# Fused attention and two MLPs on one core: weight words side by side in 8 KB places, operations over 1024 columns, output chunks later in the order of conversion

## The chip, the cores and the metric

The kernel runs on one core of a Trainium2 chip. The metric is the device time of one execution in microseconds (us), the median of several runs; less is better.

## The reference

Banded attention (window 32, for half of the heads dilated by 4) over 4 x 576 tokens with 8 heads of 64, then two feed-forward layers of 512 to 2048 to 512 over the 2304 tokens, the first with a rational function between its matrices, the second with a leaky ReLU:

```python
attn = softmax(where(mask, scale * q @ k.T, -1e9)); x = attn @ v      # per head, then side by side
h = x @ w_in;  g = P(h) / (Q(h) + 1e-6);  x = g @ w_out                 # layer 1: 512 -> 2048 -> 512
h = x @ w_in;  g = max(h, 0) + alpha * min(h, 0);  out = g @ w_out      # layer 2
```

The weights reach the chip as 64-bit floats (two 32-bit words each), so the kernel has to turn each of them into a 32-bit float first.

## The kernel before

**Tiling.** The 2304 tokens are 6 blocks (n) of 384, the 2048 hidden columns are 16 chunks (c) of 128. The unit of the first layer's loop is a pair J: two chunks of one block, so J = 0 to 7 is block 0, and there are NP = 48. For each pair TensorE forms h (`inproj`, L397, into two PSUM banks "h"), ScalarE and VectorE form g (`rat_1`, L415 to L419, which frees the bank, and `rat_2`, L425 to L430, whose last operation writes g), and TensorE adds it to the block's output (`outproj`, L448) two pairs later. Blocks 1 to 5 work with numbers split in a high and a low part (three products); block 0 works with whole f32 words and needs the weights only converted, not split. Attention runs ahead in 48 groups G, one per pair from J = 0 on, nine before the loop. The second layer follows, with a seven-product scheme over block pairs (from about 560 us on).

**Weights.** A chunk is 128 x 512 values, 128 x 1024 words of 32 bits, 4 KB in each partition. `w_load` brings the chunks of layer 1 into 16 places of 4 KB (the tags `inh0`, `outh0`, `inh2` and so on, which later hold the high parts). `w_convert` takes a pair of chunks, each in its own place, with seven operations: two Abs on ScalarE over 512 columns (L159, they read every second word), one shift on VectorE over 1024 columns (L160), two shift-and-or over 512 (L162) and two and-or over 512 (L167). The results `win`, `wout` are the f32 weights of block 0. `w_split` (L187, L188) makes high and low parts from pair J = 7 on. `w_early` converts eleven pairs of layer 2's weights during J = 16 to 42 and puts them back into DRAM.

**Order.** Nine attention groups run before the loop, and in their steps k = 3 and k = 6 one and two pairs of chunks are converted at a lower priority: in 0, then out 0 and in 2. Each of the pairs J = 0 to 6 then converts two more at its end (`w_next` twice), in the order in 0, out 0, in 2, out 2, in 4, out 4 and so on. The loads are all issued by SyncE's queue (SP), in order: the first 16 chunks before the loop, four more in each of J = 0 to 3, each as soon as the place it goes to has been converted. Every engine works through its instructions in order; a planner settles the orders from program order, priorities and expected readiness, so that an operation may stand earlier or later on its engine than in the program.

**Names.** "In 0" is the pair of input chunks 0 and 1, "out 0" the pair of output chunks 0 and 1. On the page `raw_inh`, `raw_outh` are chunks as loaded, `hl`/`gl` ends mean low parts (in block 0 `gl` is the whole g), `tc` the numerator, `ps_h` the h banks, `ps_y` the output banks.

Of the kernel before, what the change touches and what calls it, by code (L numbers as in the profile page):

```python
# [19 lines left out]
BLK = 384  # L20
# [35 lines left out]
def attn_rational_prelu_kernel(  # L56
# [58 lines left out]
    wt, raw_t, w32_t = {}, {}, {}  # L115
    src = {(1, "in"): w1_in, (1, "out"): w1_out, (2, "in"): w2_in, (2, "out"): w2_out}

    places = [f"{kind}h{c}" for c in range(0, NC, 2) for kind in ("in", "out")]
    n_raw = {1: 0, 2: 0}
    SPARE = (f"inh{NC - 2}", f"outl{NC - 4}")  # L120

    def w_load(*key):


        if key in w_dram:
            t = rawp.tile([128, 2 * DM], F32, tag="raw", name="w32")
# [3 lines left out]
        k = n_raw[key[0]]  # L130
        n_raw[key[0]] += 1
        tag = places[k % NC] if key[0] == 1 else SPARE[k % 2]
        t = wp.tile([128, 2 * DM], U32, tag=tag, name="raw_" + tag)
        nc.sync.dma_start(out=t, in_=src[key[:2]][key[2]].bitcast(U32))
        raw_t[key] = t

    def w_early(layer, kind, c):


        for i in range(2):  # L140
            t = rawp.tile([128, 2 * DM], U32, tag="raw", name="raw")
            nc.sync.dma_start(out=t, in_=src[layer, kind][c + i].bitcast(U32))
            raw_t[layer, kind, c + i] = t
        a = w_convert(layer, kind, c, f"outl{NC - 2}")
        w_dram[layer, kind, c] = dp.tile([128, 2 * DM], F32, name=f"w_dram_{kind}{c}")
        nc.sync.dma_start(out=w_dram[layer, kind, c], in_=a.bitcast(F32))

    def w_convert(layer, kind, c, tag=None):


        if layer == 1 or tag:
            a = wp.tile([128, 2 * DM], U32, tag=tag or f"{kind}l{c}", name=f"w{kind}{c}")
        else:
            a = rawp.tile([128, 2 * DM], U32, tag="u", name="u", bufs=1)
        halves = [slice(i * DM, (i + 1) * DM) for i in range(2)]
        words = [raw_t.pop((layer, kind, c + i)).rearrange("p (f t) -> p t f", t=2) for i in range(2)]
        for i in range(2):
            w32_t[layer, kind, c + i] = a[:, halves[i]]
            nc.scalar.activation(out=a[:, halves[i]].bitcast(F32), in_=words[i][:, 1, :].bitcast(F32), func=AF.Abs, scale=W_BIAS)  # L159
        nc.vector.tensor_scalar(out=a, in0=a, scalar1=3, scalar2=0, op0=ALU.logical_shift_left, op1=ALU.bitwise_or)  # L160
        for i in range(2):
            nc.vector.scalar_tensor_tensor(  # L162
                out=a[:, halves[i]], in0=words[i][:, 0, :], scalar=29, in1=a[:, halves[i]],
                op0=ALU.logical_shift_right, op1=ALU.bitwise_or,
            )
        for i in range(2):
            nc.vector.scalar_tensor_tensor(  # L167
                out=a[:, halves[i]], in0=words[i][:, 1, :], scalar=0x80000000, in1=a[:, halves[i]],
                op0=ALU.bitwise_and, op1=ALU.bitwise_or,
            )  # L170
        raw_t[layer, kind, c] = a
        return a
# [3 lines left out]
    def w_split(layer, kind, c):  # L176


        w = raw_t.pop((layer, kind, c)).bitcast(F32)
        hi = wp.tile([128, 2 * DM], F32R, tag=f"{kind}h{c}", name=f"w{kind}h{c}")  # L180
        k = c + (kind == "out")
        if k == 0 and layer == 1:
            lo = rawp.tile([128, 2 * DM], F32R, tag="u", name="winl0", bufs=1)
        else:
            tag = f"outl{NC - 2}" if k == 0 else f"inl{c}" if k % 2 else f"outl{c - 2}"
            lo = wp.tile([128, 2 * DM], F32R, tag=tag, name=f"w{kind}l{c}")
        nc.scalar.activation(out=hi, in_=w, func=AF.Copy)  # L187
# [308 lines left out]
    def stage(name):  # L496
# [7 lines left out]
    X_TAGS = {
        "B11": ("inh0", f"outl{NC - 2}"), "T2": ("inh2", "outl0"), "B21": ("inh4", "outl2"),
        "T3": ("xh0", "xl0"), "T1": ("xh0", "xl0"), "T4": ("xh1", "xl1"), "B22": ("xh1", "xl1"),
    }
    W_TAGS = (("inh6", "outl4", "inh8", "outl6"), ("inh10", "outl8", "inh12", "outl10"))

    def sub(out, a, b):  # L510
        nc.vector.tensor_tensor(out=out, in0=a, in1=b, op=ALU.subtract)  # L511

    def x_alloc(n, name):
        pool = xp if X_TAGS[name][0][0] == "x" else wp
        st_x[n, name] = [
            pool.tile([128, 2 * BLK], F32R, tag=tag, name=f"st_{name}{s}") for tag, s in zip(X_TAGS[name], "hl")
        ]

    def x_load(n):
# [32 lines left out]
        split(*st_x[n, name], st[name])  # L552

    def st_wload(q):
        t = rawp.tile([128, 2 * DM], F32, tag="raw", name="w32")
        nc.sync.dma_start(out=t, in_=w_dram[2, "in", 2 * q])
        return t

    def st_prep(q, w):
# [8 lines left out]
        ah, al = (wp.tile([128, 2 * DM], F32R, tag=t, name="st_a") for t in tags[:2])  # L568
        sh, sl = (wp.tile([128, 2 * DM], F32R, tag=t, name="st_s")[:, :768] for t in tags[2:])
# [99 lines left out]
    def w_pairs(layer):  # L669
        return [(layer, kind, c) for c in range(0, NC, 2) for kind in ("in", "out")]  # L670

    to_convert = {1: w_pairs(1), 2: [(2, "out", c) for c in range(0, NC, 2)]}
    early = w_pairs(2)[:6] + [(2, "in", c) for c in range(6, NC, 2)]
    to_load = {
        1: [(l, k, c + i) for l, k, c in w_pairs(1) for i in range(2)],
        2: [(l, k, c + i) for l, k, c in to_convert[2] for i in range(1 if (l, k, c) in early else 2)],
    }

# [236 lines left out]
```

## Time and profile before

| | |
|---|---|
| time, median of 3 runs | 913.36 us (911.81 to 914.83) |
| the profiled execution, its own time | 911.72 us |
| its span from first to last instruction | 909.9 us |
| TensorE matmul busy | 893.2 us (98%) |
| VectorE busy | 772.8 us (85%) |
| ScalarE busy | 632.7 us (70%) |
| mean granted TensorE clock | 0.996 of full speed |

PE is TensorE's matmul stream, PEld its weight loads, DVE VectorE, ACT ScalarE, SPq the queue of SyncE that issues the DMAs. A wait is put down to the instruction that released it. A granted clock of 1.00 is 2.4 GHz, 0.50 is 1.2 GHz. Successive rows of one engine overlap by about 0.1 us, since an instruction starts before the last one's results are out; the distance from start to start is what the engine is held for.

### The profile page before, as it was taken

What the parts mean: (1) busy time and instruction counts of PE and PEld (TensorE: products, weight loads), DVE (VectorE), ACT (ScalarE), POOL (GpSimd) and SP (SyncE); (2) the same over time, 40 slices, a digit from 0 to 9 for tenths busy, and PEclk for the clock granted to TensorE, in tenths of its full rate; (3) what the DMA queues carried; (4) which work ended last, traced back from release to release, by engine and by line L of the source; (5) the groups of instructions that cost most, each with busy time, mean ns of one, the idle gap of its engine ahead of it and who ended that gap; (6) DMA issues with size and microseconds to landing.
All of it is one profiled execution on the core that took longest, in us unless ns stands there. A gap on an engine that the chain in (4) does not pass through costs nothing.

```text
span 909.9 us, 14970 instructions
## 1 busy us (share of the span) xinstructions
PE 893.2 (98%) x5682; PEld 789.9 (87%) x5682; DVE 772.8 (85%) x1297; ACT 632.7 (70%) x1357; POOL 0.2 (0%) x4
## 2 busy tenths in 40 slices
PE   7799999999999999999999999999999999999998
PEld 5465568899999999999999999898898898988896
DVE  4999999998889988999999999999986769676652
ACT  5789988778988888898787856555554537553533
POOL 0000000000000000000000000000000000000000
PEclk9899999999999999999999999999999999999999
DMA  9995112213434434442211233232231102210001
GB/s 246 375 358 191 46 44 80 66 45 113 149 115 134 132 104 141 130 157 94 88 48 47 87 124 120 92 104 86 89 116 37 34 24 81 94 47 24 1 1 69
DMA packets 37896, 93.97 MB, mean 103 GB/s; under 512 B 4672, under 2 KB 14400, under 8 KB 37824
## 3 DMA queue, kind: packets, MB, share of 16 engines
q1 hardware_dynamic: 37824, 93.02, 31.5%
q8 instruction: 44, 0.72, 0.3%
q14 instruction: 28, 0.23, 0.1%
HBM read 77.79 MB, written 15.20 MB: 102 GB/s over the span
## 4 chain that ended last, share of the span: by engine, by line
PE 91%; DVE 4%; ACT 3%; DMA 1%; issue 1%; SPq 0%; ACTq 0%
PE ps_y L448 22%; PE ps_h L397 21%; PE ps_h L586 19%; PE ps_y L467 15%; PE ps_aP L467 4%; PE ps_aS L467 4%; PE ps_aP L332 2%; PE ps_aS L247 2%; PE ps_aP L305 1%; ACT p L275 1%; DMA ld_qk<-in_qk_d_dram 1%; PE ps_aS L229 1%; DVE gl L430 0%; DVE win L167 0%; DVE win L162 0%
## 5 line engine op out<-in xcount | busy, mean ns | idle before, releaser
L397 PE MATMUL ps_h<-xh,winh 128*128 128x384 f32 x320 | 109.8, 346 | 0.0
L448 PE MATMUL ps_y<-gl,wouth 128*128 128x384 f32 x320 | 107.5, 336 | 1.3 <-DVE gl L438 1.3
L448 PE MATMUL ps_y<-gh,wouth 128*128 128x384 f32 x320 | 108.3, 343 | 0.1
L448 PE MATMUL ps_y<-gh,woutl 128*128 128x384 f32 x320 | 107.1, 335 | 0.0
L397 PE MATMUL ps_h<-xl,winh 128*128 128x384 f32 x320 | 106.9, 335 | 0.0
L397 PE MATMUL ps_h<-xh,winl 128*128 128x384 f32 x320 | 106.9, 335 | 0.0
L415 ACT ACTIVATE ta<-ps_h,co 128x384 f32<-128x384 f32 x96 | 56.4, 587 | 51.8 <-PE ps_h L397 51.3
L467 PE MATMUL ps_y<-woutl,gh 128*128 128x512 f32 x192 | 76.0, 396 | 0.0
L467 PE MATMUL ps_y<-wouth,gl 128*128 128x512 f32 x192 | 75.8, 395 | 0.0
L467 PE MATMUL ps_y<-wouth,gh 128*128 128x512 f32 x192 | 74.6, 390 | 0.1
L591 ACT ACTIVATE tb<-ta 128x768 f32<-128x768 f32 x48 | 40.2, 839 | 45.3 <-DVE ta L611 44.6
L493 ACT ACTIVATE gh<-tc 128x768 fp32r<-128x768 f32 x48 | 40.3, 840 | 40.9 <-DVE st_s L511 23.7
L417 ACT ACTIVATE tc<-ps_h,co 128x384 f32<-128x384 f32 x96 | 66.1, 691 | 0.0
L397 PEld LDWEIGHTS ps_h<-xh,winh 128*128 128x128 f32 x320 | 60.0, 188 | 3.2
L448 PEld LDWEIGHTS ps_y<-gl,wouth 128*128 128x128 f32 x320 | 60.2, 188 | 1.6 <-DVE gl L438 1.5
L493 ACT ACTIVATE st_a<-w 128x1024 fp32r<-128x1024 f32 x24 | 25.4, 1058 | 50.9 <-PE ps_h L586 48.9
L397 PEld LDWEIGHTS ps_h<-xl,winh 128*128 128x128 f32 x320 | 60.1, 188 | 0.4
L448 PEld LDWEIGHTS ps_y<-gh,wouth 128*128 128x128 f32 x320 | 59.7, 188 | 0.6 <-ACT os L454 0.4
L448 PEld LDWEIGHTS ps_y<-gh,woutl 128*128 128x128 f32 x320 | 60.1, 188 | 0.0
L397 PEld LDWEIGHTS ps_h<-xh,winl 128*128 128x128 f32 x320 | 60.1, 188 | 0.0
L494 DVE TENSOR_TENSOR gl<-tc,gh 128x768 fp32r<-128x768 f32 x48 | 45.9, 956 | 16.3 <-ACT gh L493 15.6
L419 DVE SCALAR_TENSOR_TENSOR tc<-tc,co,ps_h 128x384 f32<-128x384 f32 x96 | 57.9, 615 | 0.5
(179 smaller groups left out, 2388.5 us busy)
## 6 DMA issues: line engine op xcount, KB each, us to landing
w<-w_dram_in SPq DMA_DIRECT2D x24, 512.0 KB, 3.4
ld_qk<-in_qk_d_dram SPq DMA_DIRECT2D x24, 352.0 KB, 3.9
raw<-in_w_in_dram SPq DMA_DIRECT2D x16, 512.0 KB, 4.4
ld_qk<-in_qk_p_dram SPq DMA_DIRECT2D x24, 304.0 KB, 4.1
raw_inh<-in_w_out_dram SPq DMA_DIRECT2D x13, 512.0 KB, 5.6
y_dram<-os SPq DMA_DIRECT2D x24, 192.0 KB, 2.2
out_dram<-os SPq DMA_DIRECT2D x18, 256.0 KB, 2.1
raw_inh<-in_w_in_dram SPq DMA_DIRECT2D x8, 512.0 KB, 7.9
```

Of the source, the lines that this page charges most:

```text
L247: nc.tensor.matmul(out=s[r0:r1, t * n:(t + 1) * n], lhsT=ld[:, q0:q0 + r1 - r0], rhs=ld[:, k0:k0 + n], start=False, stop=(t == T - 1),)
L332: nc.tensor.matmul(out=ot[h * 64:(h + 1) * 64, t * nq:(t + 1) * nq], lhsT=a["v"][:n, v0:v0 + 64], rhs=a["pts"][:n, t * m + h * nq:t * m + ...
L397: nc.tensor.matmul(out=hp[:, :BLK], lhsT=w, rhs=x, start=(k == 0), stop=(k == len(pairs) - 1))
L415: nc.scalar.activation(out=ta, in_=hp, func=AF.Abs, scale=co[:, 4:5])
L417: nc.scalar.activation(out=tc_, in_=hp, func=AF.Identity, scale=co[:, 3:4], bias=co[:, 2:3])
L419: nc.vector.scalar_tensor_tensor(out=tc_, in0=tc_, scalar=co[:, 1:2], in1=hp, op0=ALU.add, op1=ALU.mult)
L448: nc.tensor.matmul(out=yt[:, :BLK], lhsT=w[:, m * 128:(m + 1) * 128], rhs=g, start=(c == 0 and i == 0), stop=(c == NC - 1 and i == len(pai ...
L467: nc.tensor.matmul(out=yt, lhsT=g[:, tok], rhs=w, start=(first and i == 0), stop=(last and i == 2))
L493: nc.scalar.activation(out=hi, in_=t, func=AF.Copy)
L494: nc.vector.tensor_tensor(out=lo, in0=t, in1=hi.bitcast(F32), op=ALU.subtract)
L586: nc.tensor.matmul(out=hp, lhsT=u[:, ws], rhs=x[:, xs], start=(k == 0), stop=(k == 5))
L591: nc.scalar.activation(out=neg, in_=h, func=AF.Relu, scale=-1.0)
```

## The change

Chunks of a pair now lie side by side in one place of 8 KB (8 places instead of 16), so that `w_convert` works over the whole pair at once: one Abs, one shift, one shift-and-or, one and-or, all over 1024 columns. This holds for layer 1 (16 pairs) and for the early pairs of layer 2 (11); the five late pairs of layer 2 keep their halves. The high parts get halves of the 8 KB places (`w_place`), the two raw buffers of the early conversions become the halves of one 8 KB buffer, and one of the second layer's stages and a loading place change positions (`spare`, `W_TAGS`).

The order of conversion becomes in 0, in 2, in 4, out 0, in 6, out 2, in 8, out 4, ..., in 14, out 10, out 12, out 14. Before the loop two pairs are converted instead of three (in 0 at k = 3, in 2 at k = 6), and each of J = 0 to 6 converts two. The loads follow the same order.

```diff
-    places = [f"{kind}h{c}" for c in range(0, NC, 2) for kind in ("in", "out")]
+    places = [(kind, c) for c in range(0, NC, 4) for kind in ("in", "out")]
     n_raw = {1: 0, 2: 0}
-    SPARE = (f"inh{NC - 2}", f"outl{NC - 4}")
+    wide = {}
+
+    def w_place(kind, c, new=False, dtype=F32R):
+        if new:
+            wide[kind, c - c % 4] = wp.tile([128, 4 * DM], dtype, tag=f"{kind}H{c - c % 4}", name=f"w{kind}H{c}")
+        k = c % 4 // 2
+        return wide[kind, c - c % 4][:, k * 2 * DM:(k + 1) * 2 * DM]
+
+    def spare(k):
+        return wp.tile([128, 2 * DM], U32, tag=f"outl{NC - 6 + 2 * k}", name="spare")
+
+    def raw_half():
+        if not raw2:
+            raw2.append(rawp.tile([128, 4 * DM], U32, tag="raw", name="raw", bufs=1))
+        raw2.append(0)
+        k = len(raw2) % 2
+        return raw2[0][:, k * 2 * DM:(k + 1) * 2 * DM]
...
+        if layer == 1 and c % 2 == 0:
+            kind2, c2 = places[n_raw[1] % 8]
+            n_raw[1] += 1
+            raw_t[key] = wp.tile([128, 4 * DM], U32, tag=f"{kind2}H{c2}", name="raw_" + kind2)
+        t = raw_t[layer, kind, c - c % 2][:, c % 2 * 2 * DM:(c % 2 + 1) * 2 * DM] if layer == 1 else spare(c % 2)
+        nc.sync.dma_start(out=t, in_=src[layer, kind][c].bitcast(U32))
...
-        words = [raw_t.pop((layer, kind, c + i)).rearrange("p (f t) -> p t f", t=2) for i in range(2)]
+        if layer == 1 or tag:
+            parts = [(slice(0, 2 * DM), raw_t.pop((layer, kind, c)))]
+        else:
+            parts = [(halves[i], raw_t.pop((layer, kind, c + i))) for i in range(2)]
+        parts = [(at, w.rearrange("p (f t) -> p t f", t=2)) for at, w in parts]
         for i in range(2):
             w32_t[layer, kind, c + i] = a[:, halves[i]]
-            nc.scalar.activation(out=a[:, halves[i]].bitcast(F32), in_=words[i][:, 1, :].bitcast(F32), func=AF.Abs, scale=W_BIAS)
+        for at, w in parts:
+            nc.scalar.activation(out=a[:, at].bitcast(F32), in_=w[:, 1, :].bitcast(F32), func=AF.Abs, scale=W_BIAS)
         nc.vector.tensor_scalar(out=a, in0=a, scalar1=3, scalar2=0, op0=ALU.logical_shift_left, op1=ALU.bitwise_or)
-        for i in range(2):
+        for at, w in parts:
             nc.vector.scalar_tensor_tensor(
-                out=a[:, halves[i]], in0=words[i][:, 0, :], scalar=29, in1=a[:, halves[i]],
+                out=a[:, at], in0=w[:, 0, :], scalar=29, in1=a[:, at],
                 op0=ALU.logical_shift_right, op1=ALU.bitwise_or,
             )
...
-        hi = wp.tile([128, 2 * DM], F32R, tag=f"{kind}h{c}", name=f"w{kind}h{c}")
+        hi = w_place(kind, c, c % 4 == 0)
...
-    W_TAGS = (("inh6", "outl4", "inh8", "outl6"), ("inh10", "outl8", "inh12", "outl10"))
+    W_TAGS = ((6, "outl4", 8, "outl6"), (10, "outl8", 12, 14))
...
-    to_convert = {1: w_pairs(1), 2: [(2, "out", c) for c in range(0, NC, 2)]}
+    first = sorted(w_pairs(1), key=lambda p: p[2] + (4.5 if p[1] == "out" else 0))
+    to_convert = {1: first, 2: [(2, "out", c) for c in range(0, NC, 2)]}
...
-        1: [(l, k, c + i) for l, k, c in w_pairs(1) for i in range(2)],
+        1: [(l, k, c + i) for l, k, c in first for i in range(2)],
...
         if k in (3, 6):
             with tc.high_priority(-100):
-                for _ in range(k // 3):
-                    w_next(1)
+                w_next(1)
```

## Rows read from the trace of the kernel before

**Rows 1.** The page, busy time of TensorE: us, share, instructions

```profile
PE 893.2 (98%) x5682; PEld 789.9 (87%) x5682; DVE 772.8 (85%) x1297; ACT 632.7 (70%) x1357; POOL 0.2 (0%) x4
```

**Rows 2.** What TensorE waited for: us in total, times, longest

```profile
PE ps_h L397 <- DVE tc L419: 3.7, 1, 3.7
...
PE ps_y L448 <- DVE gl L438: 1.3, 1, 1.3
PE ps_h L397 <- DVE win L167: 1.1, 1, 1.1
PE ps_y L448 <- DVE gl L430: 1.0, 3, 0.4
```

**Rows 3.** Busy time by stretch: us, then PE, PEld, DVE, ACT, POOL, PEclk, DMA share, GB/s

```profile
24.00:50.00 26.00, 20.77 (x111) 11.89 (x109) 24.96 (x48) 19.31 (x46) 0.00 (x0) 0.87 1.03 360
50.00:118.00 68.00, 66.98 (x385) 39.62 (x385) 66.31 (x126) 62.44 (x152) 0.00 (x0) 1.00 0.51 182
118.00:163.00 45.00, 44.90 (x325) 35.65 (x321) 43.84 (x74) 36.87 (x98) 0.00 (x0) 1.00 0.24 73
...
200.00:300.00 100.00, 100.00 (x813) 95.73 (x812) 89.15 (x162) 84.46 (x225) 0.00 (x0) 1.00 0.38 121
```

**Rows 4.** VectorE in order of time, 30 to 46 us: start, us, line, operation

```profile
30.82 0.69 DVE L160 TENSOR_SCALAR wout<-wout 128x1024 uint32<-128x1024 uint32 x1 [0.25 <-ACT wout L159]
31.90 0.68 DVE L162 SCALAR_TENSOR_TENSOR wout<-raw_inh,wout 128x512 uint32<-128x512 uint32 x1
...
34.31 0.68 DVE L160 TENSOR_SCALAR win<-win 128x1024 uint32<-128x1024 uint32 x1
...
37.58 1.01 DVE L418 TENSOR_TENSOR tc<-tc,ps_h 128x384 f32<-128x384 f32 x2
38.51 1.13 DVE L419 SCALAR_TENSOR_TENSOR tc<-tc,co,ps_h 128x384 f32<-128x384 f32 x2
...
45.29 0.95 DVE L430 SCALAR_TENSOR_TENSOR gl<-tb,tc 128x768 f32<-128x768 f32 x1
```

**Rows 5.** TensorE in order of time, 33 to 50 us

```profile
33.23 2.20 PE L397 MATMUL ps_h<-xh,win 128*128 128x384 f32 x6
39.17 8.00 PE L397 MATMUL ps_h<-xh,win 128*128 128x384 f32 x16 [3.74 <-DVE tc L419]
47.01 3.39 PE L448 MATMUL ps_y<-gl,wout 128*128 128x384 f32 x10
```

**Rows 6.** TensorE by short stretches: us, busy, PEclk, DMA share, GB/s

```profile
26.00:28.00 2.00, 1.29 (x4) 1.00 1.02 397
...
36.00:37.00 1.00, 0.00 (x0) 1.00 1.01 406
...
38.00:39.00 1.00, 0.00 (x0) 0.50 1.04 414
```

**Rows 7.** The chain of work that ended last: start, us, what

```profile
24.76 1.20 DVE win L162 x2
...
29.67 1.13 ACT wout L159 x2
...
173.44 1.14 DVE woutl L188
```

**Rows 8.** ScalarE in order of time, 35 to 37 us

```profile
35.03 0.67 ACT L417 ACTIVATE tc<-ps_h,co 128x384 f32<-128x384 f32 x1
...
36.41 0.70 ACT L417 ACTIVATE tc<-ps_h,co 128x384 f32<-128x384 f32 x1
```

**Rows 9.** SP's queue: median us to landing on the page; one issue in order of time

```profile
raw_outh<-in_w_in_dram SPq DMA_DIRECT2D x8, 512.0 KB, 8.7
...
73.44 0.42 SPq L211 DMA_DIRECT2D ld_qk<-in_qk_d_dram  x1
```

**Rows 10.** VectorE in order of time, around pair 3's g

```profile
85.16 0.68 DVE L167 SCALAR_TENSOR_TENSOR wout<-raw_outh,wout 128x512 uint32<-128x512 uint32 x1
85.76 0.95 DVE L430 SCALAR_TENSOR_TENSOR gl<-tb,tc 128x768 f32<-128x768 f32 x1
```

More of the change, by code (lines that the diff above doesn't have):

```diff
@@ L116, in attn_rational_prelu_kernel @@
     src = {(1, "in"): w1_in, (1, "out"): w1_out, (2, "in"): w2_in, (2, "out"): w2_out}
-    places = [f"{kind}h{c}" for c in range(0, NC, 2) for kind in ("in", "out")]
+    places = [(kind, c) for c in range(0, NC, 4) for kind in ("in", "out")]
     n_raw = {1: 0, 2: 0}
-    SPARE = (f"inh{NC - 2}", f"outl{NC - 4}")
+    wide = {}
[12 more added lines that the diff above has]
+        return raw2[0][:, k * 2 * DM:(k + 1) * 2 * DM]
+    raw2 = []
     def w_load(*key):
+        layer, kind, c = key
         if key in w_dram:
-            t = rawp.tile([128, 2 * DM], F32, tag="raw", name="w32")
+            t = raw_half().bitcast(F32)
             nc.sync.dma_start(out=t, in_=w_dram[key])
@@ L129, in w_load @@
             return
[L130 to L135, printed above, removed]
+        if layer == 1 and c % 2 == 0:
[4 more added lines that the diff above has]
+        nc.sync.dma_start(out=t, in_=src[layer, kind][c].bitcast(U32))
+        if layer == 2:
+            raw_t[key] = t
     def w_early(layer, kind, c):
+        raw_half(), raw_half()
         for i in range(2):
-            t = rawp.tile([128, 2 * DM], U32, tag="raw", name="raw")
-            nc.sync.dma_start(out=t, in_=src[layer, kind][c + i].bitcast(U32))
-            raw_t[layer, kind, c + i] = t
+            nc.sync.dma_start(out=raw2[0][:, i * 2 * DM:(i + 1) * 2 * DM], in_=src[layer, kind][c + i].bitcast(U32))
+        raw_t[layer, kind, c] = raw2[0]
         a = w_convert(layer, kind, c, f"outl{NC - 2}")
@@ L155, in w_convert @@
         halves = [slice(i * DM, (i + 1) * DM) for i in range(2)]
-        words = [raw_t.pop((layer, kind, c + i)).rearrange("p (f t) -> p t f", t=2) for i in range(2)]
+        if layer == 1 or tag:
[3 more added lines that the diff above has]
+        parts = [(at, w.rearrange("p (f t) -> p t f", t=2)) for at, w in parts]
         for i in range(2):
             w32_t[layer, kind, c + i] = a[:, halves[i]]
-            nc.scalar.activation(out=a[:, halves[i]].bitcast(F32), in_=words[i][:, 1, :].bitcast(F32), func=AF.Abs, scale=W_BIAS)
+        for at, w in parts:
+            nc.scalar.activation(out=a[:, at].bitcast(F32), in_=w[:, 1, :].bitcast(F32), func=AF.Abs, scale=W_BIAS)
         nc.vector.tensor_scalar(out=a, in0=a, scalar1=3, scalar2=0, op0=ALU.logical_shift_left, op1=ALU.bitwise_or)
-        for i in range(2):
+        for at, w in parts:
             nc.vector.scalar_tensor_tensor(
-                out=a[:, halves[i]], in0=words[i][:, 0, :], scalar=29, in1=a[:, halves[i]],
+                out=a[:, at], in0=w[:, 0, :], scalar=29, in1=a[:, at],
                 op0=ALU.logical_shift_right, op1=ALU.bitwise_or,
             )
-        for i in range(2):
+        for at, w in parts:
             nc.vector.scalar_tensor_tensor(
-                out=a[:, halves[i]], in0=words[i][:, 1, :], scalar=0x80000000, in1=a[:, halves[i]],
+                out=a[:, at], in0=w[:, 1, :], scalar=0x80000000, in1=a[:, at],
                 op0=ALU.bitwise_and, op1=ALU.bitwise_or,
@@ L503, in attn_rational_prelu_kernel @@
     st_x, st_s, st_w, st_raw = {}, {}, {}, {}
[L504 to L507, printed above, removed]
-    W_TAGS = (("inh6", "outl4", "inh8", "outl6"), ("inh10", "outl8", "inh12", "outl10"))
+    X_LO = {"B11": f"outl{NC - 2}", "T2": "outl0", "B21": "outl2"}
+    X_HI = {"B11": 0, "T2": 2, "B21": 4}
+    X_TAGS = {"T3": ("xh0", "xl0"), "T1": ("xh0", "xl0"), "T4": ("xh1", "xl1"), "B22": ("xh1", "xl1")}
+    W_TAGS = ((6, "outl4", 8, "outl6"), (10, "outl8", 12, 14))
     def sub(out, a, b):
@@ L513, in x_alloc @@
     def x_alloc(n, name):
-        pool = xp if X_TAGS[name][0][0] == "x" else wp
+        if name in X_HI:
+            lo = wp.tile([128, 2 * BLK], F32R, tag=X_LO[name], name=f"st_{name}l")
+            st_x[n, name] = [w_place("in", X_HI[name])[:, :2 * BLK], lo]
+            return
         st_x[n, name] = [
-            pool.tile([128, 2 * BLK], F32R, tag=tag, name=f"st_{name}{s}") for tag, s in zip(X_TAGS[name], "hl")
+            xp.tile([128, 2 * BLK], F32R, tag=tag, name=f"st_{name}{s}") for tag, s in zip(X_TAGS[name], "hl")
         ]
@@ L522, in x_load @@
         if n == 0:
+            for c in (0, 4):
+                w_place("in", c, True)
             for name in ("B11", "B21"):
@@ L526, in x_load @@
         else:
-            st["B11"] = st["T2"] = wp.tile([128, 2 * BLK], F32, tag=SPARE[0], name="st_b11")
-            st["B21"] = wp.tile([128, 2 * BLK], F32, tag=SPARE[1], name="st_b21")
+            st["B11"] = st["T2"] = spare(0)[:, :2 * BLK].bitcast(F32)
+            st["B21"] = spare(1)[:, :2 * BLK].bitcast(F32)
         for name in ("T3", "T1", "T4", "B22"):
@@ L554, in st_wload @@
     def st_wload(q):
-        t = rawp.tile([128, 2 * DM], F32, tag="raw", name="w32")
+        t = raw_half().bitcast(F32)
         nc.sync.dma_start(out=t, in_=w_dram[2, "in", 2 * q])
         return t
+    st_k = []
     def st_prep(q, w):
@@ L567, in st_prep @@
         tags = W_TAGS[q % 2]
-        ah, al = (wp.tile([128, 2 * DM], F32R, tag=t, name="st_a") for t in tags[:2])
-        sh, sl = (wp.tile([128, 2 * DM], F32R, tag=t, name="st_s")[:, :768] for t in tags[2:])
+        if not st_k:
+            w_place("in", 8, True)
+        if len(st_k) == 1:
+            w_place("in", 12, True)
+        st_k.append(q)
+        ah, al, sh, sl = (
+            wp.tile([128, 2 * DM], F32R, tag=t, name="st_l") if isinstance(t, str) else w_place("in", t) for t in tags
+        )
+        sh, sl = sh[:, :768], sl[:, :768]
         split(ah, al, w)
```

## The prediction

> **What bounds the kernel now.** The page comes first: TensorE's matmuls are busy for 893.2 of 909.9 us [rows 1], so all waiting and idling together is 16.7 us. That is the most that any change outside TensorE could bring, some of it lying before the first input and after the last matmul. The list of TensorE's waits says where the rest is [rows 2]: 3.7 us in one wait for VectorE's `tc`, 1.1 for the first converted weights, three waits of together 1.0 for g of block 0, and one of 1.3 for a low part of g. Nothing else above 1.4. The table by stretch shows the place [rows 3]: from 24 to 50 us TensorE is busy for 20.8 of 26 us and VectorE for 25.0; from 50 to 118 us both are full (67.0 and 66.3 of 68), and so up to 163 us; from 200 us on TensorE is full without a break and VectorE has a tenth to spare. So the conversion of weights, which is VectorE's work, can cost or give time only up to about 200 us. The eleven early conversions of layer 2 and the new places of the second layer lie behind that, under a full TensorE: I cost them at nothing. If that cover were gone, the early pairs would give back 11 times the 0.12 us worked out below.
>
> The step that matters is the start of the loop. Pair 0's products end at about 35.4 us; pair 1's begin at 39.17, after the wait of 3.74 us [rows 5], because the h bank is read last by L419 (38.51), behind L418 at 37.58 [rows 4]. VectorE was not idle: it converted out 0 (30.82 to 34.31, with a copy between) and in 2 (34.31 to 37.58). The short stretches show a second effect [rows 6]: at 36 us the granted clock is still 1.00 (2.4 GHz), at 38 us it is 0.50 (1.2 GHz) with TensorE idle, while the broken stretch at 26 us, 0.7 of 2 us idle, left it at 1.00. So pair 1's sixteen matmul instructions took 8.00 us, where ten of the same shape took 3.39 a little later [rows 5]; at that rate sixteen take 5.4, and the low clock cost 2.6.
>
> **The change part by part.**
>
> *Wider operations.* Two of the 512-column operations hold VectorE for 1.20 us [rows 7]. The trace has no two-input operation over 1024 columns that reads every second word; the nearest is the subtraction over 1024, 1.14 us [rows 7]. Bounds: 1.20 if nothing is saved, 1.14 if the reading pattern is as free at 1024 as it seems at 512. I take 1.14. A pair has two such, so it saves 0.12 us of VectorE and 16 pairs save 1.9 (0 at the other bound). On ScalarE two Abs take 1.13 [rows 7]; one saves some tenth of a us per pair, off the path. One new condition: the single Abs needs both chunks. For chunks loaded with 8.7 us to landing [rows 9] the first of the two Abs used to start ahead; now the pair waits for its later chunk, with ScalarE's exponentials of attention queued behind. I put this at 0 to 0.4 us for in 0, absorbed by VectorE's attention work, and nothing later, since the raw chunks then lie ready.
>
> *One conversion fewer before the loop.* Out 0 goes from 30.82 to behind in 4. Its last four operations hold VectorE from 31.90 to 34.31, 2.4 us, and its shift another 0.6 [rows 4]: 3.0 us leave the path to `tc`. Not all of it is gained: L418 needs ScalarE's L417, which starts at 35.03 and holds it for 0.57 (its 0.67 less the overlap of 0.1), so L418 can start at 35.6 instead of 37.58 [rows 4, 8], 1.9 us earlier. If L419 of the first item goes ahead of L418 of the second (whose L417 starts at 36.41 [rows 8]) it is 2.4. So pair 1's products begin near 37.2, at or before the point at which the clock fell, and end near 42.6 at full clock. What is late next is out 0: TensorE's next work is pair 0's output product, which needs g of pair 0 and out 0. Before, g was done at 46.2 [rows 4], and by then VectorE had done three pairs and five pieces of the next two, 3.0 us. After, it has to do four pairs by the same point (in 0, in 2, in 4, out 0). The amount is the same but for 4 x 0.12 = 0.5, so the product can begin at 45.7 where it began at 47.01 [rows 5]: 1.3 us gained, between 0 (out 0's last piece put behind g and the next numerator) and 2.4 (out 0 ahead of in 4).
>
> *One conversion behind, up to pair 6.* At each pair VectorE has one conversion fewer behind it than before, 2.9 us, plus 0.12 per pair done; the last pair repays it, when two are due instead of one. The three waits for g, 1.0 us [rows 2], fall in this stretch and should go. After pair 6 VectorE keeps only the 1.9. The later wait of 1.3 [rows 2] hangs on a round trip from TensorE through ScalarE to VectorE, which shifts along with TensorE; I count 0 of it, 1.3 at most.
>
> *Queue of SP.* Loads go in the same queue and number. The last four chunks go to places of in 8 and out 4, which are converted in pair 2, where the old order used in 6 (pair 1) and out 6. They wait perhaps 4 us longer, and the attention load behind them (73.44 [rows 9]) goes out as much later. It is loaded two pairs ahead, some 25 us: no cost.
>
> *Shared places.* Two high parts now share a tile. That a write to one half does not wait for work on the other is to be seen in `tc`: ScalarE's second L417 starts at 36.41, before VectorE's L418 on the first half at 37.58 [rows 4, 8]. No added waits, then.
>
> The sum: 1.3 + 1.0 = 2.3 us, with bounds of 1.0 (0 + 1.0) and 4.7 (2.4 + 1.0 + 1.3). The profiled execution takes 911.7 (span 909.9 and 1.8 around it) and would take 909.4; it lies 1.6 below the median of the runs, 913.4, so as a median the forecast is 911.1, its own range 908.7 to 912.4.
>
> **The rivals.**
>
> *The gap moves, and the clock falls again.* TensorE is done with pair 1 at 42.6 and waits for out 0 until 45.7: 3.1 us, against 3.74 that brought the clock to 0.50 and 0.7 of 2 us that did not [rows 5, 6]. If it falls, the output product runs at 1.2 GHz and costs the same 2.6 us: 2.3 - 2.6 = -0.3, so 913.7. For it: the gap's size. Against it: attention products can fall into it, and pair 1 may itself begin late enough to close it. The Trainium skill, TensorE: Matmul & The Clock Gate, section HAM oscillation — how this bites in real kernels, describes kernels in which every wait for input brings the clock down anew, so that the loss is paid per wait; by that rule the time is this rival's, 913.7. That the clock does fall in a wait, the trace agrees with (0.50 at 38 us).
>
> *VectorE's lead is worth more.* If the planner fills the gap so that pair 1 starts at 36.8 and out 0 is ready when it ends, all of 2.4, 1.0 and 1.3 is had: 4.7, so 908.7. For it: 2.9 us of lead through pair 6. Against: VectorE is full up to 163 us, and only 1.9 us of its work goes.
>
> *Slower: a long piece ahead of g.* The planner sets a piece of out's conversion between L429 and L430 (85.16, before g at 85.76 [rows 10]). It holds VectorE for 0.60; a whole one holds it for 1.14, and g comes 0.54 later. TensorE waited for g in three of these pairs, so there was no slack. Over pairs 0 to 6 that is 3.8 us: 917.2. It decides if the lead at g of pair 2 is under 0.54 us. Against it: the lead of 2.9.
>
> *The change doesn't reach the path.* Two-input operations over 1024 take 1.20, and the planner had put out 0 where VectorE would have waited anyway for ScalarE's L417: 913.4.
>
> **How the numbers follow.** Forecast 0.41, gap moved 0.25, full lead 0.17, long piece 0.10, nothing 0.07. A difference of about 0.3%, 2.7 us, is what a measurement of this kernel can tell from none. Faster by more than that: the full lead, 0.17, and of the forecast's own range (1.0 to 4.7) about four tenths, 0.16: 0.33. Slower: the long piece, 0.10, and a little of the gap rival's far end: 0.12. The rest, 0.55, is within. For eight in ten the range runs from 908.0, past the full lead, to 915.0, past the moved gap, and leaves out the long piece.
>
> **What would show it.** Right: the wait of `ps_h` for `tc` falls from 3.7 to under 2; L162 appears once per pair over 1024 columns at 1.14 from start to start; no wait for L430 remains in block 0; from 200 us on the stretches are the same, shifted. Wrong: a new wait of `ps_y` for `wout` of L167 near 42 to 46 us, with a granted clock of 0.50 behind it, is the moved gap; waits for L430 of about 0.5 in each pair are the long piece; a wait in the second layer for a high part would mean that the shared places do bind.

## The result, and the profile after

The changed kernel takes 917.44 us (median of 5 runs, 916.55 to 920.14) against 911.81 us of the kernel before (5 runs, 911.49 to 914.83): 1.0056 times as long, 95% interval 1.0043 to 1.007, some 5 us slower. The prediction was 911.1 us, range 908.0 to 915.0: faster by 2.3 us.

In the profiled execution (918.32 us, span 916.5) TensorE is busy for 0.5 us more than before, and VectorE for 3.1 us less; compare [rows 1]. The page's first part:

```profile
PE 893.7 (98%) x5682; PEld 791.8 (86%) x5682; DVE 769.7 (84%) x1243; ACT 631.5 (69%) x1330; POOL 0.2 (0%) x4
```

TensorE's waits in the changed kernel (in all, how often, the longest). L427 is the input product (L397 before), L478 the output product (L448), L197 the last operation of a conversion (L167), L449 the numerator (L419), L468 the low part of g (L438), L629 a product of the second layer, L659 its copy v out of the bank:

```profile
PE ps_h L427 <- DVE win L197: 2.8, 1, 2.8
PE ps_y L478 <- DVE wout L197: 2.7, 1, 2.7
PE ps_h L427 <- DVE tc L449: 2.6, 1, 2.6
PE ps_y L478 <- DVE gl L468: 2.6, 2, 1.3
...
PE ps_h L629 <- ACT v L659: 1.1, 1, 1.1
```

Against [rows 2]: the wait for `tc` has fallen from 3.7 to 2.6 and the three waits for g of block 0 are gone, but the first wait has grown from 1.1 to 2.8, a wait of 2.7 for out 0 is new, and so are a second wait of 1.3 for a low part of g and one of 1.1 for v. The stretches show where (columns as in [rows 3] and [rows 6]):

```profile
24.00:50.00 26.00, 18.57 (x117) 10.85 (x113) 21.72 (x36) 18.45 (x41) 0.00 (x0) 0.87 1.04 362
50.00:118.00 68.00, 67.07 (x371) 40.44 (x372) 64.76 (x105) 59.47 (x138) 0.00 (x0) 0.97 0.49 176
200.00:300.00 100.00, 99.52 (x808) 95.25 (x807) 90.02 (x153) 83.92 (x219) 0.00 (x0) 1.00 0.38 122
500.00:560.00 60.00, 57.67 (x320) 55.41 (x319) 56.94 (x84) 40.53 (x61) 0.00 (x0) 1.00 0.32 100
...
28.00:30.00 2.00, 1.27 (x2) 0.50 (x2) 1.85 (x6) 1.61 (x10) 0.00 (x0) 0.50 1.02 406
40.00:42.00 2.00, 0.00 (x1) 0.00 (x0) 1.29 (x3) 1.96 (x4) 0.00 (x0) 1.00 1.04 337
52.00:54.00 2.00, 2.00 (x4) 1.09 (x4) 2.00 (x4) 0.94 (x1) 0.00 (x0) 0.50 1.03 412
```

The same stretch at the change-over to the second layer in the kernel before:

```profile
500.00:560.00 60.00, 59.91 (x330) 57.56 (x329) 57.01 (x85) 40.76 (x61) 0.00 (x0) 1.00 0.31 102
```

At the start of the loop TensorE is busy for 18.6 of 26 us where it was busy for 20.8, and the granted clock is at 0.50 (1.2 GHz) twice, from 28 us and at 52 us, where before it was once [rows 6]. VectorE, full before (25.0 of 26), is idle for 4.3 us of them. At the change-over TensorE now misses 2.3 of 60 us, where it missed 0.1.

Both kernels run the same matmuls, so the loss can be laid out in time: the n-th matmul of a line in one trace is set against the n-th of the same line in the other, and the median of the differences is taken over a stretch. The changed kernel is 0.6 us behind at 22 to 25 us (a load of attention that came later), 3.5 at 215 to 230 (the end of block 0's effects), 3.6 at 490 to 510 and 6.2 from 600 us on. So 2.9 us are lost in block 0 (3.5 less the 0.6 of the start), 0.1 between, 2.6 at the change-over. The experiments below are laid out in the same three columns, each with its own delay at 22 to 25 us taken off.

### The profile page after: what moved, and what is told of

The parts are those of the page before. It is cut to its first block, busy times and chain, and to the rows that moved or that the text cites. A ratio compares the mean times of both kernels' runs of the same rounds, so it can differ in the third digit from the quotient of the medians.

```text
span 916.5 us, 14918 instructions
## 1 busy us (share of the span) xinstructions
PE 893.7 (98%) x5682; PEld 791.8 (86%) x5682; DVE 769.7 (84%) x1243; ACT 631.5 (69%) x1330; POOL 0.2 (0%) x4
## 4 chain that ended last, share of the span: by engine, by line
PE 87%; DMA 5%; ACT 5%; DVE 1%; issue 1%; SPq 1%; ACTq 0%
PE ps_h L427 21%; PE ps_y L478 20%; PE ps_h L629 19%; PE ps_y L497 14%; PE ps_aP L497 4%; PE ps_aS L497 4%; PE ps_aS L277 2%; DMA raw_out<-in_w_out_dram 2%; PE ps_aP L362 2%; PE ps_aP L335 1%; DMA y_dram<-os 1%; DMA ld_qk<-in_qk_d_dram 1%; DMA ld_v<-in_v_d_dram 1%; DMA ld_qk<-in_qk_p_dram 1%; PE ps_aS L259 1%
## 5 line engine op out<-in xcount | busy, mean ns | idle before, releaser
L478 PE MATMUL ps_y<-gl,woutH 128*128 128x384 f32 x320 | 107.6, 336 | 2.6 <-DVE gl L468 2.6
L427 PE MATMUL ps_h<-xh,winH 128*128 128x384 f32 x320 | 109.9, 345 | 0.0
L478 PE MATMUL ps_y<-gh,woutH 128*128 128x384 f32 x320 | 107.7, 343 | 0.0
L478 PE MATMUL ps_y<-gh,woutl 128*128 128x384 f32 x320 | 107.1, 335 | 0.0
L427 PE MATMUL ps_h<-xh,winl 128*128 128x384 f32 x320 | 106.7, 334 | 0.0
L427 PE MATMUL ps_h<-xl,winH 128*128 128x384 f32 x320 | 106.7, 334 | 0.0
L497 PE MATMUL ps_y<-woutH,gl 128*128 128x512 f32 x192 | 75.9, 395 | 0.0
L497 PE MATMUL ps_y<-woutH,gh 128*128 128x512 f32 x192 | 74.5, 389 | 0.0
L478 PEld LDWEIGHTS ps_y<-gl,woutH 128*128 128x128 f32 x320 | 60.2, 188 | 3.2 <-DVE gl L468 3.1
L427 PEld LDWEIGHTS ps_h<-xh,winH 128*128 128x128 f32 x320 | 60.0, 188 | 3.2
L427 PEld LDWEIGHTS ps_h<-xl,winH 128*128 128x128 f32 x320 | 60.1, 188 | 0.1
L478 PEld LDWEIGHTS ps_y<-gh,woutl 128*128 128x128 f32 x320 | 60.1, 188 | 0.0
L427 PEld LDWEIGHTS ps_h<-xh,winl 128*128 128x128 f32 x320 | 60.0, 188 | 0.0
L478 PEld LDWEIGHTS ps_y<-gh,woutH 128*128 128x128 f32 x320 | 59.7, 188 | 0.2
L448 DVE TENSOR_TENSOR tc<-tc,ps_h 128x384 f32<-128x384 f32 x96 | 52.1, 548 | 7.9 <-ACT tc L447 7.1
```

Source lines behind the costliest of these rows:

```text
L427: nc.tensor.matmul(out=hp[:, :BLK], lhsT=w, rhs=x, start=(k == 0), stop=(k == len(pairs) - 1))
L448: nc.vector.tensor_tensor(out=tc_, in0=tc_, in1=hp, op=ALU.mult)
L478: nc.tensor.matmul(out=yt[:, :BLK], lhsT=w[:, m * 128:(m + 1) * 128], rhs=g, start=(c == 0 and i == 0), stop=(c == NC - 1 and i == len(pai ...
L497: nc.tensor.matmul(out=yt, lhsT=g[:, tok], rhs=w, start=(first and i == 0), stop=(last and i == 2))
```

## The experiments

Two theories stood at first. **T:** the wide operation on in 0 makes the first product wait for both its chunks, and the clock falls; and the 8 KB places come free later at the change-over. **R:** the new order of conversion costs the time of block 0. In the runs E1, E3 and E4 all of the change stands except what is named; E2 is the kernel before with one thing of the change. The kernel before ran again beside each group of experiments (medians 911.81 to 912.64 us), and each ratio is to those runs.

| run | what it is | median us | ratio to before (95%) | block 0 | between | change-over |
|---|---|---|---|---|---|---|
| after | the change | 917.44 | 1.0056 (1.0043 to 1.007) | +2.9 | +0.1 | +2.6 |
| E1 | in 0 narrow | 918.37 | 1.005 (1.0031 to 1.007) | +3.2 | -0.4 | +5.8 |
| E2 | before, new order alone | 911.62 | 0.999 (0.9979 to 1.0001) | -0.7 | +1.3 | +0.1 |
| E3 | old order | 917.93 | 1.0057 (1.0038 to 1.0076) | +2.2 | +1.7 | +2.9 |
| E4 | all operations narrow | 915.2 | 1.0038 (1.0025 to 1.0051) | -0.5 | +0.5 | +2.1 |
| E5 | first four conversions narrow | 914.33 | 1.0026 (1.0013 to 1.0039) | -0.8 | -0.2 | +2.6 |
| E6 | in 4 KB, out 8 KB, raw two tiles | 912.16 | 1.0001 (0.9988 to 1.0014) | -0.3 | -0.3 | +0.1 |
| E7 | in 8 KB, out 4 KB, raw two tiles | 913.41 | 1.0013 (1.0003 to 1.0022) | +0.8 | +1.4 | +0.8 |
| E8 | before, out 0 third | 912.02 | 1.0001 (0.9986 to 1.0015) | +0.3 | +1.2 | 0.0 |
| E9 | as E6, raw one tile | 914.11 | 1.0018 (1.0007 to 1.0028) | -0.1 | 0.0 | +1.0 |
| E10 | as E5, raw two tiles | 914.12 | 1.0025 (1.0014 to 1.0035) | -0.8 | +0.7 | +0.9 |
| E11 | as E6, out 0 third | 911.94 | 1.0009 (0.9996 to 1.0022) | +0.9 | -0.4 | +0.2 |
| E12 | as E6, out 0 narrow | 911.38 | 0.999 (0.998 to 1.0001) | -0.1 | +0.4 | 0.0 |

The last three columns come from one profiled execution each, and block 0 in them holds the luck of the clock (last section), about 2 us. What E2, E7, E8 and E10 lose between is for the most part one wait in attention at 271 to 273 us (1.64, 1.18, 1.33 and 1.05 us).

### Width and order: E1 to E5

E1 reads the two chunks of in 0 one by one again, in the same 8 KB tile:

```diff
-        if layer == 1 or tag:
+        if (layer, kind, c) == (1, "in", 0):
+            both = raw_t.pop((layer, kind, c))
+            parts = [(halves[i], both[:, i * 2 * DM:(i + 1) * 2 * DM]) for i in range(2)]
+        elif layer == 1 or tag:
```

> The changed kernel, but the first conversion (in 0) is made of operations over 512 columns again, one chunk after the other; all the rest as changed. Theory T: the changed kernel is 5.6 us slower for two reasons: the wide operation holds the first input product back until both chunks of in 0 are converted, and the clock falls behind that gap (2.5 to 3 us in block 0), and the 8 KB places come free later at the change-over to layer 2 (2.6 us). By T this kernel takes 914.7 us: the first product waits 1.1 us and not 2.8, the granted clock is 1.00 at 28 to 34 us, and the 2.6 us at 520 to 550 us stay. Rival R: the new order of conversion (out 0 behind in 4) costs the time of block 0, by a second gap ahead of the first output product; then this kernel takes 917.

Measured 918.37. TensorE in order of time in E1 (L430 and L481 are the two products, L200 and L463 the end of a conversion and g):

```profile
26.75 2.17 PE L430 MATMUL ps_h<-xh,win 128*128 128x384 f32 x6 [0.57 <-DVE win L200]
...
47.26 1.65 PE L481 MATMUL ps_y<-gl,wout 128*128 128x384 f32 x2 [3.78 <-DVE gl L463]
```

The first product is back at 26.75, with a wait of 0.57 (T said 1.1), and no time came of it: TensorE's wait moved to the first output product, 3.78 us, with the clock at 0.50 behind it. That is the second gap that R named, and R's 917 is nearer than T's 914.7: T is wrong in that in 0 alone would do. The runs of E1 lie far apart, 915.4 to 921.0, the fastest with a mean clock of 0.998 and the profiled one, the slowest, with 0.990; its 5.8 us at the change-over hold waits of 1.5 and 2.3 us and a low clock behind them (0.97 over 500 to 560 us). So E1 by itself says little of what in 0 alone is worth.

E2 is the kernel before with the order alone:

```diff
-    to_convert = {1: w_pairs(1), ...}
+    first = sorted(w_pairs(1), key=lambda p: p[2] + (4.5 if p[1] == "out" else 0))
+    to_convert = {1: first, ...}
...
-                for _ in range(k // 3):
-                    w_next(1)
+                w_next(1)
```

> The kernel before with the new order of conversion alone (in 0, in 2, in 4, out 0, ..., two conversions before the loop), operations over 512 columns, 4 KB places. Theory T: the order by itself is worth little either way, 910.5 to 913.3 us, and the change-over to layer 2 is that of the kernel before. Rival R, the order costs the time of block 0: 914.5 to 915.

Measured 911.62, within the span that T gave; R falls. TensorE in order of time:

```profile
36.97 5.43 PE L397 MATMUL ps_h<-xh,win 128*128 128x384 f32 x16 [2.04 <-DVE tc L419]
45.89 2.93 PE L448 MATMUL ps_y<-gl,wout 128*128 128x384 f32 x4 [3.49 <-DVE wout L167]
```

and the stretch that begins with the second of these:

```profile
46.00:48.00 2.00, 2.00 (x4) 1.09 (x5) 2.00 (x5) 0.81 (x2) 0.00 (x0) 0.50 1.07 260
```

Pair 1 starts 2.2 us earlier than before [rows 5] and at full clock, and then TensorE waits 3.49 us for out 0, with the clock at 0.50 behind that.

E3 is the changed kernel with the old order (the lines of E2 the other way round).

> The changed kernel (wide operations, 8 KB places) with the order of conversion of the kernel before (in 0, out 0, in 2, ..., three conversions before the loop). Theory T: the gap ahead of the first product and the late places stay, so 916 to 918 us. Rival R, the order costs the time of block 0: 914.5 to 915.

Measured 917.93, as T said and not R. The first product waits 2.79 us for in 0, as in the changed kernel.

E4 takes the operations back to 512 columns everywhere (E1's edit for every pair of layer 1 and the early ones of layer 2), places and order as changed.

> The changed kernel, with all operations of the conversion over 512 columns again: the 8 KB places and the new order remain. Theory T: block 0 goes back to that of the kernel before and the late places stay, so 914.5 us. Rival R, the order costs the time of block 0: 917. If the wide operations save what the forecast said, it is some 0.5 us slower than the changed kernel with in 0 alone narrow.

Measured 915.2: between T and R, nearer T. Block 0 is back to the kernel before, the change-over is not. E1 and E4 together say that wide operations do cost block 0, but not through in 0 alone. So two new theories: W1, only the conversions at the start of the loop matter; W2, a wide operation delays something in every pair.

E5 makes the first four conversions narrow (`if (layer, kind, c) in first[:4]` in E1's edit), the other twelve wide.

> The changed kernel with the first four conversions (in 0, in 2, in 4, out 0) made of operations over 512 columns, the other twelve over 1024. The runs so far: the wide operations cost 2.2 us (917.4 against 915.2 with all narrow), and with in 0 alone narrow the time did not come back, since the clock fell in a longer wait of the first output product. Theory W1: the wide operations cost only at the start of the loop (24 to 60 us), where VectorE's order decides when each gap ends and whether the clock falls behind it; later they save their 0.06 each. Then this kernel is at 914.5 to 915.2, with TensorE idle and slow as with all narrow up to 157 us. Theory W2: a wide operation delays whatever waits behind it in every pair; then 916.5 or more.

Measured 914.33, just under the range of W1, with block 0 at -0.8: W1 stands. TensorE in order of time:

```profile
26.09 2.17 PE L430 MATMUL ps_h<-xh,win 128*128 128x384 f32 x6 [1.14 <-DVE win L200]
36.85 5.43 PE L430 MATMUL ps_h<-xh,win 128*128 128x384 f32 x16 [2.04 <-DVE tc L452]
```

The first four wide conversions cost, by the two ratios, 0.3% or some 2.7 us; the twelve later ones nothing that shows. How the 2.7 us divide among in 0, in 2, in 4 and out 0 is not told apart, but E1 against E5 shows one more way than the wait for in 0. VectorE in E1, then in E5 (L195 shift-and-or of in 4, L452 the numerator that pair 1 waits for):

```profile
36.25 1.22 DVE L195 SCALAR_TENSOR_TENSOR win<-raw_in,win 128x1024 uint32<-128x1024 uint32 x1
37.39 0.60 DVE L452 SCALAR_TENSOR_TENSOR tc<-tc,co,ps_h 128x384 f32<-128x384 f32 x1
```

```profile
35.59 0.69 DVE L195 SCALAR_TENSOR_TENSOR win<-raw_in,win 128x512 uint32<-128x512 uint32 x1
36.19 0.61 DVE L452 SCALAR_TENSOR_TENSOR tc<-tc,co,ps_h 128x384 f32<-128x384 f32 x1
```

The whole of the operation stands ahead of the numerator in E1, one half of it in E5, and pair 1 waits 2.57 us in E1 and 2.04 in E5.

### Places: E6, E7, E9, E10

What remained in E5 is the change-over. Three things of the change reach it: the high parts of in in 8 KB places, those of out, and the raw buffer as one tile of 8 KB. E6 takes the first and the third back, and with them the conversions of in and the early ones to 512 columns; the changed positions (`spare`, `W_TAGS`) stay:

```diff
     def w_place(kind, c, new=False, dtype=F32R):
+        if kind == "in":
+            return wp.tile([128, 2 * DM], dtype, tag=f"inh{c}", name=f"w{kind}h{c}")
...
-            t = raw_half().bitcast(F32)
+            t = rawp.tile([128, 2 * DM], F32, tag="raw", name="w32")
```

> The changed kernel's order; in parts back in 4 KB places and converted by operations over 512 columns; out parts in 8 KB places, converted over 1024; the raw buffer of the early conversions back to two tiles. Theory P: the 2.1 to 2.9 us at the change-over to layer 2 come from places of in that come free only after four chunks have been read; then the change-over is that of the kernel before (no wait for v, shift at 620 us equal to that at 500 us) and the time 911 to 912.5. Rival: the 8 KB places of out, or the changed places of the second layer's parts, cost it; then the wait for v remains and the time is 913.5 to 915.

E7 is its counterpart: in alone at 8 KB, with the same edit for `kind == "out"`, the two raw tiles, and all operations narrow.

> The changed kernel's order with all operations over 512 columns; in parts in 8 KB places, out parts and raw buffers in 4 KB ones. Theory P: the places of in alone bring the loss at the change-over, 2.1 to 2.9 us, with the waits for g and for v at 527 to 546 us, so 913.5 to 915. Rival (places of out or the raw buffer): 911.5 to 912.3, with the change-over of the kernel before.

E6 measured 912.16 and +0.1 at the change-over, E7 913.41 and +0.8, with a wait of 0.6 for g and none for v. So the places of in are a part, but not the 2.1 to 2.9 that theory P gave them. The changed positions, which E6 keeps, cost nothing that shows. E9 puts the one raw tile back into E6, E10 takes it out of E5; the early conversions become wide and narrow with it:

> As the run with in in 4 KB places (in narrow in 4 KB places, out wide in 8 KB places, the changed order of conversion), but with the one raw tile of 8 KB that the changed kernel has, and its wide early conversions of layer 2. So far: in places of 8 KB alone bring 0.8 us at the change-over to layer 2, without the wait for v; with out and raw at 8 KB too it is 2.1 to 2.9. If the raw tile is the rest, the wait for v (about 1 us at 540 to 546 us) is back, the change-over costs 1.3 to 2.1 us and the time is 913.4 to 914.3. If it takes in and out places of 8 KB together, the change-over is that of the kernel before and the time 911.5 to 912.5.

> The changed kernel with the first four conversions narrow (measured: 914.3, of it 2.6 us at the change-over) and the raw buffer back in two tiles of 4 KB, so that the early conversions of layer 2 are narrow too; in and out places stay at 8 KB. If the raw tile is the rest of the loss at the change-over, it falls to the 0.8 us of the in places and the time is 912.3 to 913; if in and out places together are, it stays at 2.6 us and 914.3.

E9 has +1.0 at the change-over, with a wait of 0.6 for g: the raw tile alone is about as much as the places of in alone. E10 has +0.9, as E7: with the raw tile gone, 8 KB places of out on top of those of in add nothing. The wait for v (0.8 to 2.3 us) comes only where both stand (after, E1, E3, E4, E5). E4 points to the tile and not to the width of the early conversions: they are narrow there, on the one tile, and it has +2.1 where E10, narrow on two tiles, has +0.9. But E10's median, 914.12, stands above the 912.3 to 913 expected, and its ratio, 1.0025, is that of E5, 1.0026; its profiled execution had begun 0.9 us late and lost another 0.7 between block 0 and the change-over. Why its time did not follow the change-over stays open: by the times alone the raw tile shows in E9 against E6 (1.0018 and 1.0001) and not in E10 against E5.

What the two do is seen on ScalarE and VectorE. First the split of B11, a block of the second layer's input whose high part goes to a place of in, on ScalarE, in the kernel before, in the changed one, in E7 (in 8 KB) and in E9 (raw one tile):

```profile
460.11 0.88 ACT L493 ACTIVATE st_B11h<-st_B11l 128x768 fp32r<-128x768 f32 x1
```

```profile
472.59 0.87 ACT L523 ACTIVATE winH<-st_B11l 128x768 fp32r<-128x768 f32 x1
```

```profile
473.45 0.86 ACT L529 ACTIVATE winH<-st_B11l 128x768 fp32r<-128x768 f32 x1
```

```profile
458.92 0.88 ACT L528 ACTIVATE winh<-st_B11l 128x768 fp32r<-128x768 f32 x1
```

With in in 8 KB places that split comes 12 to 13 us later, of which 3.6 in the changed kernel and 1.7 in E7 are the delay that they had by then. It fits that the place of in 0 is free only when in 2, which shares it, has been read for the last time too, a pair later; that this sets the order is not shown apart from the fit. With the raw tile it is not later; there the split of the second layer's first in weights comes earlier (490.45 on VectorE in E9, 502.30 in E6). Both end in the same thing, on VectorE in the kernel before (the last two low parts of g of the first layer, and a split of the second layer's out weights):

```profile
521.15 0.95 DVE L438 TENSOR_TENSOR gl<-tc,gh 128x768 fp32r<-128x768 f32 x1
525.82 1.22 DVE L188 TENSOR_TENSOR woutl<-w,wouth 128x1024 fp32r<-128x1024 f32 x1
526.95 0.95 DVE L438 TENSOR_TENSOR gl<-tc,gh 128x768 fp32r<-128x768 f32 x1
```

and in the changed kernel, which is 3.6 us behind at that point:

```profile
516.69 1.22 DVE L218 TENSOR_TENSOR woutl<-raw,woutH 128x1024 fp32r<-128x1024 f32 x1
528.51 0.95 DVE L468 TENSOR_TENSOR gl<-tc,gh 128x768 fp32r<-128x768 f32 x1
529.85 0.95 DVE L468 TENSOR_TENSOR gl<-tc,gh 128x768 fp32r<-128x768 f32 x1
```

In E7 and in E9 the same two lines:

```profile
514.81 1.22 DVE L224 TENSOR_TENSOR woutl<-w,wouth 128x1024 fp32r<-128x1024 f32 x1
525.98 0.95 DVE L474 TENSOR_TENSOR gl<-tc,gh 128x768 fp32r<-128x768 f32 x1
```

```profile
505.13 1.22 DVE L223 TENSOR_TENSOR woutl<-raw,woutH 128x1024 fp32r<-128x1024 f32 x1
523.25 0.95 DVE L473 TENSOR_TENSOR gl<-tc,gh 128x768 fp32r<-128x768 f32 x1
```

In E6 they stand as before (g at 519.81, the split at 524.48). VectorE is nearly full there (57.0 and 56.9 of 60 us), so a piece of the second layer that the planner puts ahead takes the place of g: the g before the last comes 7.4 us later than before, of which 3.6 are the delay so far, and TensorE waits for it. The wait for v follows from it. TensorE and ScalarE in the changed kernel:

```profile
529.52 0.44 PE L478 MATMUL ps_y<-gl,woutH 128*128 128x384 f32 x1 [1.25 <-DVE gl L468]
...
546.66 0.44 PE L629 MATMUL ps_h<-winH,winH 128*128 128x384 f32 x1 [1.08 <-ACT v L659]
```

```profile
546.12 0.49 ACT L659 ACTIVATE v<-ps_h 128x384 f32<-128x384 f32 x1 [1.55 <-DMA y_dram<-os]
```

ScalarE's v waits 1.55 us for the DMA that writes the first layer's last outputs away, since v and those outputs take turns in the same two buffers; the late g has made the outputs late. Why the planner orders the splits otherwise with one raw tile than with two was not found: both let the same loads take turns in the same bytes.

### A kernel better than both: E8, E11, E12

E8 is E2 with out 0 one place earlier (2.5 in place of 4.5 in the key: in 0, in 2, out 0, in 4, ...).

> The kernel before with another order of conversion: in 0, in 2, then out 0, in 4, out 2, in 6 and so on, two conversions ahead of the loop; operations over 512 columns, 4 KB places. With out 0 behind in 4 (measured: 911.6) the wait ahead of pair 1 fell to 2.0 us but a wait of 3.5 us for out 0 came after it, with the clock at 0.50 behind it. If that is the whole loss of that order, then with out 0 third both waits are short, the clock stays at 1.00, and the time is 908.5 to 910. If the chain of ScalarE and VectorE to g sets the end of that wait and not out 0, it stays near 911.5.

Measured 912.02. The second wait fell to 1.7 us, now for g and not for out 0, and the clock stayed at 1.00 from 24 to 60 us, as expected; then one wait of 1.6 for g at 136 us and one of 1.3 in attention at 272 us took it back. E11 is the same order in the form of E6, E12 is E6 with out 0 narrow:

> In narrow in 4 KB places, out wide in 8 KB places, two raw tiles, and the order in 0, in 2, out 0, in 4, out 2. The attempt at a kernel better than both: with out 0 behind in 4, this form waited 4.4 us for out 0 with the clock at 0.50 behind it; out 0 third kept the clock at 1.00 in the narrow form. If the clock stays up here too and nothing else comes up, 909 to 911; if the wide piece of out 0 ahead of g costs what it saves, 912.

> The form with in narrow in 4 KB places and out wide in 8 KB places (measured 912.2; it waited 4.4 us for out 0), with out 0 narrow too, so that only the seven later conversions of out are wide. If a wide out 0 lengthens that wait, it falls back to the 3.5 us of the order alone, and the time is 910.7 to 911.6: that of the order alone (911.6) less at most 7 times 0.12 = 0.8 us for the wide operations. If the wide operations save nothing that reaches TensorE, it is 911.6 to 912.2.

E11 measured 911.94: the waits are 2.6 and 2.2 and the clock falls behind the second. E12 measured 911.38, 0.999 of the kernel before; its wait for out 0 is 3.49 again, where E6 with out 0 wide waited 4.42. A wide out 0 so costs 0.9 us of waiting, and seven wide conversions of out gain nothing that shows over E2. No version is faster than the kernel before by more than the intervals.

## Why the prediction was wrong

**The wider operations.** The duration was right: 1.13 us from start to start (L192 at 25.80, the next operation at 26.93) against the 1.14 taken. What was mis-sized is the readiness. The step said that a wide operation needs both chunks to be loaded, "0 to 0.4 us for in 0", and stopped there. It needs both to be converted as well before anyone reads the first: before, the first product started at 26.71 when chunk 0's half was done; now VectorE's one operation runs from 27.37 to 28.59, behind an attention reduction, and the product starts at 28.73, with the clock at 0.50. VectorE and TensorE in the kernel before:

```profile
25.88 0.68 DVE L167 SCALAR_TENSOR_TENSOR win<-raw_inh,win 128x512 uint32<-128x512 uint32 x1
26.71 2.17 PE L397 MATMUL ps_h<-xh,win 128*128 128x384 f32 x6 [1.14 <-DVE win L167]
```

VectorE, then TensorE, in the changed kernel:

```profile
25.80 1.22 DVE L192 SCALAR_TENSOR_TENSOR win<-raw_in,win 128x1024 uint32<-128x1024 uint32 x1
...
27.37 1.22 DVE L197 SCALAR_TENSOR_TENSOR win<-raw_in,win 128x1024 uint32<-128x1024 uint32 x1
...
32.87 0.69 DVE L190 TENSOR_SCALAR win<-win 128x1024 uint32<-128x1024 uint32 x1 [1.96 <-ACT win L189]
```

```profile
28.73 1.62 PE L427 MATMUL ps_h<-xh,win 128*128 128x384 f32 x2 [2.78 <-DVE win L197]
...
50.76 0.91 PE L478 MATMUL ps_y<-gl,wout 128*128 128x384 f32 x2 [2.70 <-DVE wout L197]
```

The last line of VectorE shows the second half of it: VectorE, which the prediction took for full, then sat idle for 1.96 us, since ScalarE's Abs stood behind attention work that the slow TensorE delayed. "Absorbed by VectorE's attention work" was the wrong step: the first four wide conversions cost some 2.7 us (E5) instead of at most 0.4. What part of that is in 0's alone is not known, since E1 did not win it back.

**One conversion fewer.** With narrow operations the working holds nearly to the number: pair 1 forecast at 37.2, 36.97 in E2 (which was 0.6 us early at 22 to 25 us); its sixteen matmuls at 5.4, 5.43; out 0's product at 45.7, 45.89. But the gap ahead of that product, forecast as 3.1 us, is 3.49, and the clock falls. That is the rival "the gap moves", which had 0.25 against the forecast's 0.41; it priced the order at 0.3 us slower in the profiled execution, and E2's ends 0.1 behind. The order by itself is then worth 0.6 us or nothing (0.999, interval to 1.0001).

**The three waits for g** went in the changed kernel and in E2, as forecast. E2's gain in block 0 is 0.7 us with them, and it is lost again at about 270 us to one wait of 1.6 in attention.

**What was counted as nothing.** "The eleven early conversions of layer 2 and the new places of the second layer lie behind that, under a full TensorE: I cost them at nothing." This is the costliest wrong step beside the first: 2.6 us at the change-over. TensorE is full there in the kernel before (59.91 of 60 us), and so is VectorE (57.0). The argument looked at the length of the work, which hardly changes, and not at when its places come free. The step "Shared places ... No added waits, then" was read from two halves of a tile that is in use; when the whole of a tile comes free for its next user was not asked. The text named the right thing to look for, places that bind in the second layer, but expected it as a wait for a high part; it came as waits for g and for v.

**The rivals.** The slower rival's time, 917.2, is near the measured one by luck: its mechanism did not happen, since there is no wait for L460 (L430 before) in the changed kernel. The sign of the moved gap, "a new wait of `ps_y` for `wout`" with the clock at 0.50 behind it, did come, at 50.76 and not at 42 to 46, together with a growth of the first wait and the loss at the change-over, which no rival held.

**The 1.3 us wait for g** that hangs on a round trip stayed at 1.3, as forecast, in every kernel but E1 and E3.

**Two sums.** The forecast added 1.6 us to the profiled execution to come to the median of three runs, 913.4; the median of five is 911.81, so that term was scatter. And the 16.7 us, called the most that a change outside TensorE could bring, leave out what a low clock adds to TensorE's busy time, 2.6 us by the prediction's own rows.

## What to carry to other kernels

Two operations made into one save little here (0.07 us: 1.13 against 1.20), and join two points in time: price the first reader of the first half, at the place where the pipeline starts and nothing is ahead. Places made into one can come free later than each would alone, and in a planned program that can reorder work hundreds of microseconds on, where an engine without slack must give way (0.8 to 2.9 us here); so go through every later user of a place that the change merges. A conversion moved off one gap of a full engine is late at the next one.

## What the runs showed of the hardware

The same wait did not always bring the clock down. In E2, E5, E6, E7, E8 and E12 pair 1 waited 2.04 us and its sixteen matmuls then took 5.43 us; in E4, E9 and E10 the wait was the same 2.04 us, behind the same work (from 27 to 38 us TensorE's rows in E4 and E8 start within 0.02 us of each other), and they took 7.12. TensorE in E4, in order of time, and then a stretch of it:

```profile
37.72 7.12 PE L430 MATMUL ps_h<-xh,win 128*128 128x384 f32 x16 [2.04 <-DVE tc L452]
```

```profile
38.00:40.00 2.00, 2.00 (x4) 1.02 (x4) 2.00 (x4) 1.87 (x4) 0.00 (x0) 0.50 1.02 407
```

In the changed kernel a wait of 2.63 us left the clock at 1.00 (40 to 42 us), and waits of 2.78 and 2.70 did not. A fall costs 1.7 us here and 2.6 in the kernel before (8.00 for the same sixteen, [rows 5]). One kernel alone shows it too: of the ten runs of E11, whose waits are 2.6 and 2.2 us, six took 911.5 to 912.1 us with a mean clock of 0.998, and four took 914.7 to 915.2 with 0.993 to 0.996 (where in those it was low is not recorded). So what gaps of 2 to 3 us cost, as in the changed kernel, is in good part a matter of luck in each execution. The Trainium skill, TensorE: Matmul & The Clock Gate, section HAM oscillation — how this bites in real kernels, describes a kernel in which every wait for the next input, of some 3 to 5 us, brings the clock down. The traces agree for the seven waits of 3.49 to 4.42 us (before, E1, E2, E5, E6, E7, E12), which all have 0.50 in them or just behind; of the shorter ones some have and some have not.
